# Attention and a routed MLP on one core: half-seen key tiles made in quarters of the array and packed into shared columns

## The chip, the cores and the metric

The kernel runs on one core of one Trainium2 chip. The metric is the device time of one execution in microseconds, the median of three runs. Engines are named as the profile names them: PE (TensorE, matmuls; its weight loads are PEld), DVE (VectorE), ACT (ScalarE), POOL (GpSimd) and SP (SyncE, which issues DMAs).

## What is computed

The first half is causal attention by blocks of 64: a query sees every key of its own block and of the blocks before it. There are 8 batches of 8 heads, 576 positions (9 blocks) and 64 dimensions.

```python
scores = scale * np.matmul(q, k.transpose(0, 1, 3, 2))
mask = block_i >= block_j
scores = np.where(mask, scores, -1000000000.0)
scores = scores - np.max(scores, axis=-1, keepdims=True)
attn = np.exp(scores)
attn = attn / (np.sum(attn, axis=-1, keepdims=True) + 1e-09)
return np.matmul(attn, v).astype(np.float32)
```

The second half takes the 4608 rows of 512 numbers that result. A gate chooses one of 8 experts for each row (a second, local gate can let a row keep the expert of the row before it), and the row goes through that expert's two matrices with a ReLU between, times the gate's share. The change touches the attention only.

## The kernel before

**Work items.** The attention walks over 32 pairs of heads (one batch, two heads). The two heads of a pair lie side by side: head 0's dimensions on partitions 0 to 63, head 1's on 64 to 127. So a matmul of queries and keys uses 64 rows of the array, and the two heads' matmuls run in its two row halves at the same time.

**Two sorts of scores.** For each pair the scores are made twice. First in bf16 with queries on partitions (`top`, three jobs: middle, high, low blocks), only for each query's maximum, which DVE takes from PSUM (L594, L597, L599). The maxima, negated, go on diagonals `diag` (L613, L620; one block of 64 columns for each block of queries). Then in f32 with keys on partitions: `products` (L650) makes scores transposed, and `less` (L659) subtracts each query's maximum by a matmul of `ones` with `diag`. `expo` (L666) takes the exponential on ACT into `prob`, and `av` (L684, L692) multiplies `prob` with V, two column halves of the array at a time, 65 columns each (64 of V, and a column of ones that gives the sum).

**Segments.** Keys come in five tiles of 128 (the last of 64). Key tile j needs only queries from 128 j on, so its columns number 576, 448, 320, 192 and 64: 1600 for each head. `SEGS` packs them into four segments, one PSUM tile of two banks each (one bank for each head). An entry is (key tile, first query, number, column): segment 0 holds tile 1 and tile 4, segment 1 the first 256 queries of tile 0 and tile 3, segment 2 tile 2, segment 3 the rest of tile 0. `place(j, q0)` finds a column in `prob` again.

**Half-seen tiles.** The first 64 queries of key tiles 0 to 3 belong to an even block, whose queries see only the first half of the tile's 128 keys. Before the change the whole tile is computed, and `corners` (L676) then sets the lower half of these 64 columns to zero, with four POOL memsets for a pair.

**Order of the work.** The order on every engine is written out by hand, in one loop over `it`. In one pass of it pair e = `it` gets its last two segments and V's products, pair c = e + 1 its middle and high maxima and its first two segments, pair a = e + 2 is transposed (`turns`, L987), and pair x = e - 1 has its result normalized (`norm`, L543, L544) and transposed (`halves_x`, L712). PE's order in one pass is: middle scores of c, segments 3 and 2 of e, turns of a, high scores of c, products of c's segments 0 and 1, transposes of x's result and of a's last block (L1044), low scores of a, subtractions for c (L659), V's products of e.

**PSUM tiles.** Three tiles of two banks serve all scores and segments; `seg_tile(place)` asks for one of three places. Places 1 and 2 change roles after every pass (`ring`). Place 0 holds c's middle scores and then c's segment 0, so these products wait until DVE has taken the middle maximum. Two single banks (`g_tile`) hold transposes and V's results; ACT copies the transposes out (L1053, L716, L720) before V's products take the bank again.

POOL holds, in its own order: exchanges of maxima (L607 to L609), low diagonals (L613), casts of queries into `qh` (L1028, L1069, L1072), the memsets, a cast of the result (L515) and the issues of the weights' DMAs (L63).

Of the kernel before, what the change touches and what calls it, by code (L numbers as in the profile page):

```python
# [16 lines left out]
def kernel(  # L17
# [11 lines left out]
    nc = tc.nc  # L29
# [16 lines left out]
    P = 128  # L46
# [352 lines left out]
    def slots(inv, tok_g, tok_s):  # L399
# [4 lines left out]
        if tok_s is not None:  # L404
# [13 lines left out]
    def place(j, q0):  # L418
        for s, parts in enumerate(SEGS):
# [18 lines left out]
    with tc.manual_schedule():  # L438
# [188 lines left out]
        def mid_maxima(i, where):  # L627
            top(i, 1, where)
            exchange(i, slice(5, 6), slice(6, 7), slice(12, 13))
            if i > 1:  # L630
                first_shift(i)

        def high_maxima(i, where):
# [6 lines left out]
            if i <= 1:  # L640
                first_shift(i)
# [20 lines left out]

        def expo(i, ps, s):
            p = prob[i % 2]
            w = sum(x[2] for x in SEGS[s])
            nc.scalar.activation(p[:, :, SEG0[s]:SEG0[s] + w], ps[:, :, 0:w],  # L666
                                 func=AF.Exp, scale=scale_attn)
            if s < 2:
                corners(i, s)

        def corners(i, s):
            p = prob[i % 2]
            for (j, a, n, c) in SEGS[s]:
                if j < 4 and a == 128 * j:
                    cc = SEG0[s] + c
                    nc.gpsimd.memset(p[64:128, :, cc:cc + 64], 0.0)  # L676

        def av(i, g, m):
# [9 lines left out]
            for h in range(2):  # L688
                for j in range(m + 1):
                    for e in range(2):  # L690
                        c = place(j, 128 * m + 64 * e)
                        nc.tensor.matmul(g[rows(e), o + 65 * h:o + 65 * h + 65],  # L692
                                         lhsT=p[:, h, c:c + 64], rhs=t[:, j, h, :],
# [279 lines left out]
        for it in range(-2, NPR):  # L973
# [24 lines left out]
            def segment(s, where):  # L998
                ps = seg_tile(where)
                products(e, ps, s, 0)  # L1000
                less(e, ps, s, 0)
                expo(e, ps, s)
# [27 lines left out]
            def tails():  # L1030

                tail = nat[:, 8].rearrange("p h d -> p (h d)") if on_a else None
                if on_x:
                    if it < NPR - 2:
                        g0, g1 = gx = g_tile(0), g_tile(1)
                    else:
                        ps = seg_tile(1 if on_c else 0)
# [45 lines left out]
            if it == -2:  # L1083
# [5 lines left out]
                top(0, 2, 1)  # L1089
                low_exchange(0)  # L1090
                weights(2)
                mid_maxima(0, 2)
# [3 lines left out]
                products(0, opened, 0, 1)  # L1096
                high_maxima(0, 1)
                continue

            if on_x:  # L1100
# [6 lines left out]
            if it == 0:  # L1107
                segment(3, 1)
                mid_maxima(c, 0)
                turns()  # L1110
                segment(2, 2)
            elif on_e:
                if on_c:
                    mid_maxima(c, 0)
                run(it, "mid")
                segment(3, 1)
                segment(2, 2)
# [18 lines left out]
            if on_e:  # L1136
                corners(e, 2)
            run(it, "begin")
            if on_c and not on_e:
                ps0, ps1 = opened, seg_tile(2)  # L1140
                for z in range(2):
                    products(c, ps1, 1, z)
                top(a, 2, 1)
# [262 lines left out]
```

## Time and profile before

| | us |
|---|---|
| runs: median of 3 (lowest, highest) | 452.41 (451.03, 453.89) |
| the profiled execution's own time | 456.63 |
| its span in the profile | 454.9 |
| start of the attention's last product with V (L692) | 304.6 |
| three ordinary pairs, 60.96 to 86.51 | 8.52, 8.52, 8.51 |

The granted clock was 0.996 of full speed over the span. In a timeline row the columns are start, duration of the merged group, engine, line, operation, tiles written and read, shapes, count, and in brackets the idle time of the engine before it with what ended it. A line of the profile that begins with a time range gives for each engine its busy time in that window and the number of its instructions, then the clock, the DMA share and GB/s. Matmuls of different parts of the array overlap, so their durations don't add; the distances between starts do.

### The profile page before, as it was taken

Reading aid. Unit: us, or ns where it says so; the run is one execution under the profiler, and the core shown is the slowest. Engines: PE = TensorE matmul, PEld = TensorE weight load, DVE = VectorE, ACT = ScalarE, POOL = GpSimd, SP = SyncE. Lnnn points to the kernel's source line nnn. Section 1 sums busy time; section 2 is a strip of 40 time slices with the busy share of each in tenths; the row PEclk is TensorE's granted clock in tenths of the full one; section 3 lists DMA queues with packets and bytes.
Section 4 is the critical chain, followed back from the end, with each engine's and each line's share of the span. In section 5 each row is a group of like instructions: output and inputs, shape, how many; then the busy total and the mean of one; then the engine's idle time right before and its main releaser. Section 6 shows DMA issues by size and latency. Waiting matters only on the chain. (4 is left out here: it accounts for less than half of the span.)

```text
span 454.9 us, 19769 instructions
## 1 busy us (share of the span) xinstructions
PE 429.3 (94%) x7780; PEld 338.4 (74%) x7802; DVE 316.4 (70%) x843; ACT 271.5 (60%) x573; POOL 295.5 (65%) x700
## 2 busy tenths in 40 slices
PE   7899899999999999899999999999999999999994
PEld 5688688878787877788778887786776676766772
DVE  4777667768778788887899998866865873333322
ACT  3856666766567757775777576454554553553552
POOL 4556466657556666887566788654877767667652
PEclk8999999999999999999999999999999999999999
DMA  7999799899999987999889998857545545555551
GB/s 153 187 164 173 138 177 184 157 186 171 184 171 171 170 167 149 194 157 180 172 167 178 163 192 145 143 107 161 139 131 154 143 124 155 146 123 156 138 122 66
DMA packets 169887, 71.18 MB, mean 156 GB/s; under 512 B 151424, under 2 KB 158080, under 8 KB 169792
## 3 DMA queue, kind: packets, MB, share of 16 engines
q1 hardware_dynamic: 154640, 38.05, 43.3%
q0 software_dynamic: 13952, 31.52, 34.4%
q8 instruction: 65, 1.06, 1.0%
q10 hardware_dynamic: 1200, 0.30, 0.3%
q14 instruction: 30, 0.25, 0.2%
HBM read 67.18 MB, written 14.97 MB: 181 GB/s over the span
## 5 line engine op out<-in xcount | busy, mean ns | idle before, releaser
L666 ACT ACTIVATE prob<-ps_s 128x640 f32<-128x640 f32 (+2 forms) x128 | 103.7, 839 | 44.1 <-PE ps_s L659 42.9
L594 DVE TENSOR_REDUCE mx<-ps_m 128x2 f32<-128x640 f32 (+2 forms) x96 | 100.3, 1044 | 17.5 <-PE ps_m L589 6.4
L650 PE MATMUL ps_s<-plb 64*128 64x320 f32 (+4 forms) x768 | 104.9, 394 | 1.2 <-DVE mx L597 0.9
L650 PEld LDWEIGHTS ps_s<-plb 64*128 64x128 f32 x768 | 69.2, 188 | 22.5 <-issue 11.1
L692 PE MATMUL g<-vt,prob 128*64 128x65 f32 x2560 | 81.1, 222 | 0.5 <-issue 0.4
L692 PEld LDWEIGHTS g<-vt,prob 128*64 128x64 f32 x2560 | 77.9, 138 | 1.0 <-issue 0.9
L827 ACT ACTIVATE hT<-ps_h 128x512 bf16<-128x512 f32 x76 | 43.9, 596 | 42.5 <-PE ps_h L823 28.4
L838 PE MATMUL ps_o<-w_bf,hT 128*128 x282 | 67.1, 379 | 1.4 <-issue 0.3
L838 PEld LDWEIGHTS <-hT 128*128 128x128 bf16 x304 | 28.0, 98 | 27.9 <-issue 0.3
L804 DVE COPY natb<-w_bf 128x4096 bf16 x20 | 24.7, 1236 | 30.9 <-PE ps_h L823 23.7
L841 ACT ACTIVATE o_sb<-ps_o,share 128x512 f32<-128x512 f32 x37 | 25.4, 687 | 29.5 <-PE ps_o L838 12.0
L804 DVE COPY plb<-w_bf 128x4096 bf16 x20 | 24.7, 1234 | 23.3 <-PE ps_h L823 13.7
L823 PEld LDWEIGHTS <-plb 128*128 128x128 bf16 x608 | 35.4, 98 | 7.0 <-issue 2.9
L823 PEld LDWEIGHTS <-natb 128*128 128x128 bf16 x608 | 35.4, 98 | 7.0 <-issue 2.3
L659 PE MATMUL ps_s<-diag,ones 64*128 64x448 bf16 (+1 forms) x372 | 36.7, 274 | 1.1 <-DVE diag L613 0.6
L63 POOL DMA_DIRECT2D w_bf<-in_moe_w_dram x56 | 34.1, 608 | 1.5 <-DMA x_rows<-xb 0.4
L1023 ACT COPY plb<-g 128x512 f32<-128x512 f32 x62 | 33.2, 593 | 1.2 <-PE g L987 1.2
L607 POOL COPY mx<-mx 64x2 f32<-64x2 f32 x64 | 11.7, 183 | 33.7 <-DVE mx L594 32.2
L676 POOL MEMSET prob<- 64x128 f32 x128 | 24.3, 205 | 13.1 <-ACT prob L666 7.6
L847 POOL DMA_INDIRECT out_dram<-o_sb,tok2s x17 | 19.0, 1117 | 20.0 <-ACT o_sb L841 10.9
L568 PE MATMUL ps_m<-kh,qh 64*128 64x320 bf16 (+2 forms) x192 | 25.7, 309 | 3.3 <-POOL qh L1028 1.2
L684 PEld LDWEIGHTS g<-vt,prob 128*64 128x64 f32 x640 | 21.4, 137 | 9.7 <-ACT xT L720 4.6
(291 smaller groups left out, 803.7 us busy)
## 6 DMA issues: line engine op xcount, KB each, us to landing
w_bf<-in_moe_w_dram POOLq DMA_DIRECT2D x48, 256.0 KB
vt<-in_v_dram SPq DMA_DIRECT2D x64, 128.0 KB
natb<-in_k_dram SPq DMA_DIRECT2D x63, 128.0 KB
natb<-in_q_dram SPq DMA_DIRECT2D x63, 128.0 KB
w_bf<-in_moe_w_dram POOLq DMA_DIRECT2D x8, 512.0 KB
x_rows<-w_bf SPq DMA_DIRECT2D x13, 256.0 KB
natb<-in_k_dram SPq DMA_DIRECT2D x32, 32.0 KB
vt<-in_v_dram SPq DMA_DIRECT2D x32, 32.0 KB
```

The costliest lines, as they stand in the source:

```text
L63: nc.gpsimd.dma_start(out=dst[:, e * WE:(e + 1) * WE].rearrange("p (k f) -> p k f", k=n)[:, r:r + m, :], in_=view[e][:, r:r + m, :])
L568: nc.tensor.matmul(ps[:, h, c:c + w], lhsT=qh[rows(h), 64 * b:64 * b + 128], rhs=kh[rows(h), 0:w], start=True, stop=m is None)
L594: nc.vector.reduce_max(mx[:, 7:12:4] if job == 0 else mx[:, b:b + 2], ps[:, :, 0:w], axis=AX)
L650: nc.tensor.matmul(ps[:, h, c:c + n], lhsT=pls[i][rows(h), S + 128 * j:S + 128 * j + 128], rhs=pls[i][rows(h), a:a + n], start=part == 0, ...
L659: nc.tensor.matmul(ps[:, h, c:c + n], lhsT=ones[rows(h), :], rhs=diag[rows(h), a // 64:(a + n) // 64, :], start=False, stop=part == len(SE ...
L666: nc.scalar.activation(p[:, :, SEG0[s]:SEG0[s] + w], ps[:, :, 0:w], func=AF.Exp, scale=scale_attn)
L692: nc.tensor.matmul(g[rows(e), o + 65 * h:o + 65 * h + 65], lhsT=p[:, h, c:c + 64], rhs=t[:, j, h, :], start=(j == 0), stop=(j == m))
L804: nc.vector.tensor_copy(w, w1_bf[:, bass.ds(off, WE)])
L823: nc.tensor.matmul(ps_h[:, f, :], lhsT=w[:, f0 + ko * F:f0 + ko * F + 2 * P - 1:2], rhs=xb[:, ko * P:(ko + 1) * P], start=(ko == 0), stop= ...
L827: nc.scalar.activation(hT[:, half * 4:half * 4 + 4, :], ps_h, func=AF.Relu)
L838: nc.tensor.matmul(ps_o, lhsT=hT[:, fo, :], rhs=w2_bf[:, bass.ds(woff + fo * Dm, Dm)], start=(fo == 0), stop=(fo == FO - 1))
L1023: nc.scalar.copy(pl[:, w * S:w * S + 512], pw[w])
```

## The change

`SEGS` has three segments instead of four, of 512, 512 and 448 columns for each head (1472 in all). The half-seen first 64 queries of key tiles 0 to 3 are no longer part of them. Blocks 0, 2, 4 and 6 are instead computed as 64 keys by 64 queries (`products_halves`, `less_halves`): blocks 0 and 2 write partitions 0 to 63, blocks 4 and 6 partitions 64 to 127, so that 0 and 4 share 64 columns and 2 and 6 the next 64 (`HALVES` lists block, half and column). With two heads in two row halves that is four quarters of the array.

V's products must then take from such a column only the half that belongs to their block. They use `vh`, a copy of V whose other half is zero: `halves_v` fills it for each pair with two POOL copies, at the start of the pass; there is one `vh` for all pairs. The memsets of `corners` are gone.

The halves are computed at the start of a pass, behind the V products of the pair before and ahead of the middle scores of c; the rest of segment 2 follows after these, in the same PSUM tile. `first_shift`, which makes the diagonal of block 0, moves for every pair to the end of `high_maxima`. The places of the three PSUM tiles change so that they need no exchange after every pass.

```diff
-    SEGS = [[(1, 128, 448, 0), (4, 512, 64, 448)],
-            [(0, 0, 256, 0), (3, 384, 192, 256)],
-            [(2, 256, 320, 0)],
-            [(0, 256, 320, 0)]]
-    SEG0 = [448, 0, 960, 1280]
-    WP = 1600
+    SEGS = [[(0, 64, 512, 0)],
+            [(1, 192, 384, 0), (3, 448, 128, 384)],
+            [(2, 320, 256, 0), (4, 512, 64, 384)]]
+    HALVES = [(0, 0, 256), (4, 1, 256), (2, 0, 320), (6, 1, 320)]
+    SEG0 = [0, 512, 1024]
+    WP = 1472
...
+        vh = const([P, 4, 2, D + 1], F32, "vh")
+        nc.gpsimd.memset(vh, 0.0)
+        for z in range(2):
+            nc.gpsimd.memset(vh[64 * z:64 * z + 64, 2 * z:2 * z + 2, :, D:D + 1], 1.0)
...
         def mid_maxima(i, where):
             top(i, 1, where)
             exchange(i, slice(5, 6), slice(6, 7), slice(12, 13))
-            if i > 1:
-                first_shift(i)
...
             shift(i, 7, 2, nc.vector)
-            if i <= 1:
-                first_shift(i)
+            first_shift(i)
...
+        def products_halves(i, ps):
+            for b, z, c in HALVES:
+                for h in range(2):
+                    nc.tensor.matmul(ps[rows(z), h, c:c + 64],
+                                     lhsT=pls[i][rows(h), S + 64 * b:S + 64 * b + 64],
+                                     rhs=pls[i][rows(h), 64 * b:64 * b + 64],
+                                     start=c == 256, stop=False)
+
+        def less_halves(i, ps):
+            diag = diag1 if i else diag0
+            for b, z, c in HALVES:
+                for h in range(2):
+                    nc.tensor.matmul(ps[rows(z), h, c:c + 64], lhsT=ones[rows(h), 0:64],
+                                     rhs=diag[rows(h), b, :], start=False, stop=c > 256)
...
-        def corners(i, s):
-            p = prob[i % 2]
-            for (j, a, n, c) in SEGS[s]:
-                if j < 4 and a == 128 * j:
-                    cc = SEG0[s] + c
-                    nc.gpsimd.memset(p[64:128, :, cc:cc + 64], 0.0)
+        def halves_v(i):
+            for z in range(2):
+                nc.gpsimd.tensor_copy(vh[rows(z), 2 * z:2 * z + 2, :, 0:D],
+                                      vt[i % 2][rows(0), 2 * z:2 * z + 2, :, 0:D])
...
-                                         lhsT=p[:, h, c:c + 64], rhs=t[:, j, h, :],
+                                         lhsT=p[:, h, c:c + 64],
+                                         rhs=(t if e or j < m else vh)[:, j, h, :],
...
+            if on_e:
+                halves_v(e)
...
             elif on_e:
+                ps = halves(1)
                 if on_c:
                     mid_maxima(c, 0)
                 run(it, "mid")
-                segment(3, 1)
-                segment(2, 2)
+                segment(ps)
...
-                    high_maxima(c, 1)
+                    high_maxima(c, 2)
...
-            if on_e:
-                corners(e, 2)
...
             if on_c and on_e:
-                ps0, ps1 = seg_tile(0), seg_tile(2)
+                ps0, ps1 = seg_tile(0), seg_tile(1)
                 products(c, ps0, 0, 0)
                 for z in range(2):
                     products(c, ps1, 1, z)
-                products(c, ps0, 0, 1)
```

PE's order in an ordinary pass, from the end of V's products to the next pair's products. `g` is a bank of V's results or transposes, `ps_m` scores for maxima, `ps_s` a segment. Of rows that come once for each head one is shown. Before:

```order
L692 MATMUL g_891<-vt_149,prob_147 64x65 x24
L583 MATMUL ps_m<-kh,qh 128x64
L589 MATMUL ps_m<-kh,qh 128x384
L650 MATMUL ps_s<-plb 128x320 x2
L659 MATMUL ps_s<-diag,ones 128x320
L987 MATMUL g_953<-id_f,natb 128x64
L568 MATMUL ps_m<-kh,qh 128x512
L650 MATMUL ps_s<-plb 128x448 x2
L650 MATMUL ps_s<-plb 128x256 x2
L650 MATMUL ps_s<-plb 128x192 x2
L650 MATMUL ps_s<-plb 128x64 x2
```

The rows of L650 and L659 with 320 columns come twice there, once for segment 3 and once for segment 2. After:

```order
L670 MATMUL ps_s<-plb 64x64 x8
L679 MATMUL ps_s<-diag,ones 64x64
L590 MATMUL ps_m<-kh,qh 128x64
L596 MATMUL ps_m<-kh,qh 128x384
L654 MATMUL ps_s<-plb 128x256 x2
L654 MATMUL ps_s<-plb 128x64 x2
L663 MATMUL ps_s<-diag,ones 128x256
L1003 MATMUL g_988<-id_f,natb 128x64
L575 MATMUL ps_m<-kh,qh 128x512
L654 MATMUL ps_s<-plb 128x512 x2
L654 MATMUL ps_s<-plb 128x384 x2
L654 MATMUL ps_s<-plb 128x128 x2
```

The halves (eight products, eight subtractions of L679) now stand between V's products and the middle scores; one segment of 320 columns is gone, and the next pair's products have three parts and 1024 columns instead of four parts and 960.

DVE's order in the same stretch, from the normalization of the result (`x<-g`) to the low maxima. Before:

```order
L543 RECIPROCAL rs<-g_1280 128x6
L544 TENSOR_TENSOR x<-g_1280,rs 128x384
L594 TENSOR_REDUCE mx<-ps_m 128x2
L599 TENSOR_REDUCE mx<-ps_m 128x2
L620 TENSOR_TENSOR diag<-negi,mx 64x64 x2
L594 TENSOR_REDUCE mx<-ps_m 128x2
L636 TENSOR_REDUCE mx<-mx 64x1
L637 COPY mx<-mx 64x1
L638 TENSOR_REDUCE mx<-mx 64x1
L613 TENSOR_TENSOR diag<-negi,mx 128x128
L594 TENSOR_REDUCE mx<-ps_m 128x2
```

After:

```order
L550 RECIPROCAL rs<-g_1317 128x6
L551 TENSOR_TENSOR x<-g_1317,rs 128x384
L601 TENSOR_REDUCE mx<-ps_m 128x2
L606 TENSOR_REDUCE mx<-ps_m 128x2
L601 TENSOR_REDUCE mx<-ps_m 128x2
L641 TENSOR_REDUCE mx<-mx 64x1
L642 COPY mx<-mx 64x1
L643 TENSOR_REDUCE mx<-mx 64x1
L620 TENSOR_TENSOR diag<-negi,mx 128x128
L627 TENSOR_TENSOR diag<-negi,mx 64x64 x2
L601 TENSOR_REDUCE mx<-ps_m 128x2
```

The two instructions for block 0's diagonal moved from between the middle and the high maximum to behind the high blocks' diagonal.

More of the change, by code (lines that the diff above doesn't have):

```diff
@@ L996, in weights, with halves, segment @@
                     n -= m
-            def segment(s, where):
+            def halves(where):
                 ps = seg_tile(where)
-                products(e, ps, s, 0)
-                less(e, ps, s, 0)
-                expo(e, ps, s)
+                products_halves(e, ps)
+                less_halves(e, ps)
+                return ps
+            def segment(ps):
+                for z in range(2):
+                    products(e, ps, 2, z)
+                for z in range(2):
+                    less(e, ps, 2, z)
+                expo(e, ps, 2)
             def turns():
@@ L1221 @@
                 keep_sums(x, ge)
-            if on_e:
-                ring[1:] = ring[:0:-1]
         att.close()
```

30 lines of the change are left out of this document (15 added, 15 removed).

## The prediction

> **What bounds the kernel now.** I read the engines' shares first, then the busy time of one ordinary pair of heads by windows, then the timeline of that pair for each engine. The page's first row:
>
> ```profile
> PE 429.3 (94%) x7780; PEld 338.4 (74%) x7802; DVE 316.4 (70%) x843; ACT 271.5 (60%) x573; POOL 295.5 (65%) x700
> ```
>
> TensorE (PE) looks full, but matmuls overlap and their ends are modelled, so the share alone proves little. The window of one ordinary pair of the attention, and PE's timeline in it:
>
> ```profile
> 69.48:78.00 8.52, 8.41 (x192) 7.04 (x186) 6.31 (x16) 5.94 (x13) 5.73 (x19) 1.00 1.08 187
> ```
>
> ```profile
> 68.80 0.87 PE L692 MATMUL g<-vt,prob 128*64 128x65 f32 x24
> 69.60 0.23 PE L583 MATMUL ps_m<-kh,qh 64*128 64x64 bf16 x4
> 69.67 0.19 PE L589 MATMUL ps_m<-kh,qh 64*128 64x64 bf16 x2
> 69.70 0.19 PE L563 MATMUL ps_m<-ones,unseen 64*128 64x64 bf16 x2
> 69.73 0.33 PE L589 MATMUL ps_m<-kh,qh 64*128 64x384 bf16 x2
> 69.89 0.70 PE L650 MATMUL ps_s<-plb 64*128 64x320 f32 x4
> 70.43 0.30 PE L659 MATMUL ps_s<-diag,ones 64*128 64x320 bf16 x2
> 70.57 0.70 PE L650 MATMUL ps_s<-plb 64*128 64x320 f32 x4
> ...
> 71.24 0.66 PE L987 MATMUL g<-id_f,natb 64*128 64x64 f32 x16
> 71.73 0.38 PE L568 MATMUL ps_m<-kh,qh 64*128 64x512 bf16 x2
> 71.95 1.84 PE L650 MATMUL ps_s<-plb 64*128 64x448 f32 x16
> 73.63 0.48 PE L712 MATMUL g<-id_f,x 64*128 64x64 f32 x10
> 73.94 0.23 PE L1044 MATMUL g<-id_f,natb 64*128 64x64 f32 x2
> ...
> 75.05 0.80 PE L684 MATMUL g<-vt,prob 128*64 128x65 f32 x20
> 75.69 2.50 PE L692 MATMUL g<-vt,prob 128*64 128x65 f32 x80
> 78.12 0.23 PE L583 MATMUL ps_m<-kh,qh 64*128 64x64 bf16 x4
> ```
>
> Starts are what counts here. From start to start: middle scores 0.29 us (69.60 to 69.89), segment 3 0.68, segment 2 0.67, turns 0.49, high scores 0.22, the next pair's products 1.68, turned results 0.31, then 1.11 to V's products, which take 3.07 until the next pair. I call 69.60 time 0 of the pair: products start at 2.35, L712 at 4.03, V's products at 5.45, the next pair at 8.52. PE is the bound nearly everywhere, with one wait inside that PE's speed can't shorten:
>
> ```profile
> 75.05 0.66 PEld L684 LDWEIGHTS g<-vt,prob 128*64 128x64 f32 x20 [0.37 <-ACT xT L720]
> ```
>
> ```profile
> 74.24 0.27 ACT L1053 COPY plb<-g 128x128 f32<-128x128 f32 x1 [0.55 <-PE g L1044]
> ...
> 74.79 0.21 ACT L720 COPY xT<-g 64x64 f32<-64x64 f32 x1
> ```
>
> V's products wait for a chain of ACT copies that starts only when L1044 is done. So the 1.11 us after L1044 are fixed, and the top scores and the subtractions in it (L659 of the next pair's segments) have 0.37 us to spare: 64 columns more there, about 0.03 us, cost nothing.
>
> The second thing to see is how close VectorE (DVE) stands behind PE:
>
> ```profile
> 69.72 0.20 DVE L543 RECIPROCAL rs<-g 128x6 f32<-128x6 f32 x1 [0.56 <-PE g L692]
> ...
> 70.42 1.08 DVE L594 TENSOR_REDUCE mx<-ps_m 128x2 f32<-128x896 f32 x1
> 71.42 0.28 DVE L599 TENSOR_REDUCE mx<-ps_m 128x2 f32<-128x128 f32 x1
> ```
>
> The next pair's products at 71.95 go into the PSUM tile (place 0) that these two maxima read, and L599 ends at 71.70: slack of a quarter of a microsecond. In a pair where the maxima came later, PE did wait:
>
> ```profile
> 233.81 1.08 DVE L594 TENSOR_REDUCE mx<-ps_m 128x2 f32<-128x896 f32 x1
> 234.81 0.28 DVE L599 TENSOR_REDUCE mx<-ps_m 128x2 f32<-128x128 f32 x1
> ```
>
> ```profile
> 235.15 0.30 PEld L650 LDWEIGHTS ps_s<-plb 64*128 64x128 f32 x4 [0.27 <-DVE mx L599]
> 235.63 0.19 PEld L650 LDWEIGHTS ps_s<-plb 64*128 64x128 f32 x2 [0.18 <-issue]
> ```
>
> From the start of L594 to the first product are 235.15 - 233.81 = 1.34 us, and the first pass then takes 0.48 instead of 448 x 0.84 ns = 0.38, since its weights were not loaded ahead: 0.10 on top. The view of the products' tile counts four such waits before the change:
>
> ```profile
>   DVE mx L599: 1.5, 4
> ```
>
> **The change, part by part.** Prices first. A pass of 320 f32 columns by both heads at once is half of 70.43 - 69.89 = 0.54, or 0.84 ns a column; bf16 takes 70.57 - 70.43 = 0.14 for 320, or 0.43 ns.
>
> *Removed:* segment 3 (0.68), and of segment 2's 0.67 what shrinks: now 256 + 64 columns, twice 320 x 0.84 = 0.54, and 0.14 to subtract. To that 0.07 for the narrow part: the 960 columns at 71.95 should take 1.61 and take 1.68, and I put the rest down to the 64-column part, whose weights are as wide as any (an estimate). That part moves to segment 2. Segment 2 then costs 0.75.
>
> *Added:* the halves, 8 f32 matmuls (16 passes) and 8 bf16 of 64 columns, in quarters of the array. No row shows a 64x64 quarter. The two-at-a-time step is known: V's products, 65 columns, take 0.058 each two ((0.87 - 0.22) / 11 from the first row), and 64 bf16 columns 0.03. One at a time would be 16 x 0.058 + 8 x 0.03 = 1.17 us, two at a time 0.58, four at a time 4 x 0.058 + 2 x 0.03 = 0.29. The nearest row is the gate's sums, which put four column groups into the array:
>
> ```profile
> 95.22 0.63 PE L757 MATMUL g<-xT,wgl 128*32 128x128 f32 x14
> ...
> 95.98 0.53 PE L757 MATMUL g<-scr,wgl 128*32 128x128 f32 x6
> 96.44 0.23 PE L583 MATMUL ps_m<-kh,qh 64*128 64x64 bf16 x4
> ```
>
> Between the first and the last row shown stand 32 passes, 16 of 160 and 16 of 128 columns. Two at a time they would need 1.94 us (288 x 16 x 0.84 / 2); they took 1.22. So four do run together, and the two heads' row groups do as well: I take 0.29 and keep 0.58 for the range.
>
> *Changes of the array's shape.* V's last 24 passes at 68.80 need 12 x 0.059 = 0.71 and the next start is 69.60: 0.10 lost when the shape goes from 128x64 to 64x128. The halves put a third shape between, so this is paid twice: 0.10 more (bounds 0 and 0.10). [...] The first f32 step after a change also costs 0.05 (20 passes at 75.05 take 0.64, ten steps of 0.059 are 0.59).
>
> *What that makes of a pair.* Halves from 0 to 0.05 + 0.29 = 0.34; change, so middle scores at 0.44. How soon can DVE take their maximum? At 70.42 it was DVE that was late, with its normalization. Where DVE was free:
>
> ```profile
> 96.94 1.09 DVE L594 TENSOR_REDUCE mx<-ps_m 128x2 f32<-128x896 f32 x1 [0.89 <-PE ps_m L589]
> ```
>
> That is 0.50 after the scores' start at 96.44. So the maximum starts at the later of 0.82 (DVE free, 70.42) and 0.44 + 0.50 = 0.94: PE now is late by 0.12. Products at 0.94 + 1.34 = 2.28, plus 0.10 for weights not ahead, in effect 2.38 against 2.35. PE itself would have been ready at 0.44 + 0.29 + 0.75 + 0.49 + 0.22 = 2.19, so the columns that were saved turn into a wait of 0.09 and the 0.10 behind it. The products are now 512 + 384 + 128 = 1024 columns, 2 x 1024 x 0.84 = 1.72, without the 0.07. L712 starts at 4.10 against 4.03: a pair takes 0.07 us longer. Bounds: with maxima at 0.82 (shape changes free) products at 2.26, a pair 0.05 shorter; with halves at 0.58, 0.36 longer.
>
> *Hidden or small.* The exponentials fall from 3200 to 2944 columns and from four to three instructions a pair; ACT waits for PE there and gives nothing back:
>
> ```profile
> 70.77 1.44 ACT L666 ACTIVATE prob<-ps_s 128x640 f32<-128x640 f32 x2 [1.96 <-PE ps_s L659]
> ```
>
> POOL loses four memsets (three take 0.66) and gains two copies of 64x256, bounded by its rows of 128 and 640 columns:
>
> ```profile
> 71.64 0.18 POOL L607 COPY mx<-mx 64x1 f32<-64x1 f32 x1 [1.20 <-DVE mx L594]
> ...
> 73.24 0.61 POOL L1028 CAST qh<-plb 128x512 bf16<-128x512 f32 x1
> ...
> 75.47 0.30 POOL L1072 CAST qh<-plb 128x128 bf16<-128x128 f32 x1
> ...
> 76.29 0.73 POOL L515 CAST w_bf<-x 128x640 bf16<-128x640 f32 x1
> 77.08 0.66 POOL L676 MEMSET prob<- 64x128 f32 x3
> ```
>
> 0.30 to 0.73 each, 0.4 by size. They wait for V's last product of the pair before, since they overwrite `vh`, and block POOL's queue so long: behind them stands L607, which waits for DVE until 71.64 anyway (1.20 idle), so 0.8 us is covered. Where POOL makes one-hot rows in that gap (two pairs) I count 0.2 each. Block 0's diagonal (two DVE instructions) leaves the path from middle to high maximum, which helps only where PE waited for the diagonal, as here:
>
> ```profile
> 183.53 0.59 PE L659 MATMUL ps_s<-diag,ones 64*128 64x448 bf16 x8 [0.30 <-DVE diag L613]
> ```
>
> I allow 0.2 each for two such pairs, beyond what the fixed ACT chain would hold PE for anyway (an estimate); it cancels POOL's 0.4. No DMA is added; only weights' issues on POOL come earlier by the memsets. First and last pairs cancel within 0.3.
>
> **Sum.** 29 pairs x 0.07 = +2.0 us on a profiled span of 454.9 (the run itself took 456.6). That is +0.4%; carried to the median of the runs, 452.4 + 2.0 = 454.4.
>
> **The rivals.** *B, slower: quarters go two at a time.* Then halves take 0.58, scores start at 0.73, the maximum at 1.23, and a pair grows by 0.36: 29 x 0.36 = 10.4, 462.8 us. It decides once the halves take over 0.38 us (0.16 a pair, 29 of which make 4.6). For it: no row mixes row and column groups. Against it: L757. [...]
>
> *C, the saving arrives.* If products need not wait for the maximum, they start at 2.19 and a pair loses 2.35 + 1.68 - 2.19 - 1.72 = 0.12: 29 x 0.12 = 3.5, 448.9 us. Against it stands the wait at 235.15, on this very tile.
>
> *D, POOL takes over.* L1028 ends at 73.85 and top scores start at 74.00; with maxima 0.12 later it ends at 73.97 and PE wants it at 74.07. Another 0.2 us on POOL would show fully: 0.17 a pair, 29 x 0.17 = 4.9, 457.3 us.
>
> **How the numbers follow.** My forecast 0.58, B 0.19, C 0.10, D 0.13. The forecast's own range runs from -0.05 to +0.16 a pair, 450.9 to 457.0. Eight in ten over all: 449.0 to 462.5. A measurement of this kernel can tell about 1% from no change. Faster by over 1% (below 447.9) needs more than C gives: 0.07. Slower by over 1% (above 456.9): B, over half of D and the edge of the forecast, 0.30. Within 1%: 0.63.
>
> **What would show it.** Right: a row of PEld at the next pair's products that waits for the DVE maximum in nearly every pair (instead of four); middle maxima waiting for PE; halves that span about 0.3 us of starts; 0.1 us between shapes; an ordinary pair of 8.55 to 8.6 us. Wrong: a pair under 8.45, or no wait at the products; halves over 0.38 us; top scores that wait for POOL's `qh` in every pair.

## The result, and the profile after

| | before | after |
|---|---|---|
| runs, us: median (lowest to highest) | 452.32 (451.03 to 453.89), 4 | 464.77 (463.72 to 466.45), 4 |
| ratio, 95% interval | | 1.0293 (1.0253 to 1.0333) |
| profiled execution, its span | 456.63, 454.9 | 466.45, 464.7 |
| three ordinary pairs | 8.52, 8.52, 8.51 | 8.67, 8.67, 8.67 |

The change makes the kernel 2.9% slower, 12.4 us; the forecast was 454.4, and 462.5 the end of its range. From the page after, the engines' shares and three of the DMA queues (packets, MB, share of 16 engines):

```profile
PE 434.3 (93%) x8356; PEld 343.4 (74%) x8378; DVE 318.2 (68%) x843; ACT 261.1 (56%) x541; POOL 300.8 (65%) x639
...
q1 hardware_dynamic: 154640, 38.05, 43.2%
q0 software_dynamic: 13952, 31.52, 34.1%
q8 instruction: 69, 1.13, 1.1%
```

ACT has become 10 us less busy and PE is busy 5 us longer, with 576 matmuls and 576 weight loads more. An ordinary pair, PE in the timeline (from the halves on; rows of single matmuls left out):

```profile
83.24 0.46 PE L670 MATMUL ps_s<-plb 64*64 64x64 f32 x16
83.52 0.24 PE L679 MATMUL ps_s<-diag,ones 64*64 64x64 bf16 x8
83.70 0.23 PE L590 MATMUL ps_m<-kh,qh 64*128 64x64 bf16 x4
...
83.99 0.76 PE L654 MATMUL ps_s<-plb 64*128 64x256 f32 x8
84.58 0.30 PE L663 MATMUL ps_s<-diag,ones 64*128 64x256 bf16 x4
84.72 0.69 PE L1003 MATMUL g<-id_f,natb 64*128 64x64 f32 x16
85.25 0.38 PE L575 MATMUL ps_m<-kh,qh 64*128 64x512 bf16 x2
85.63 2.00 PE L654 MATMUL ps_s<-plb 64*128 64x512 f32 x12
87.43 0.50 PE L728 MATMUL g<-id_f,x 64*128 64x64 f32 x10
87.73 0.26 PE L1067 MATMUL g<-id_f,natb 64*128 64x64 f32 x2
...
88.84 0.80 PE L699 MATMUL g<-vt,prob 128*64 128x65 f32 x20
```

The same pair on DVE, and PE's weight loads at the next products:

```profile
84.19 1.09 DVE L601 TENSOR_REDUCE mx<-ps_m 128x2 f32<-128x896 f32 x1
85.20 0.28 DVE L606 TENSOR_REDUCE mx<-ps_m 128x2 f32<-128x128 f32 x1
```

```profile
85.60 0.33 PEld L654 LDWEIGHTS ps_s<-plb 64*128 64x128 f32 x4 [0.30 <-PE g L1003]
86.13 0.22 PEld L654 LDWEIGHTS ps_s<-plb 64*128 64x128 f32 x2 [0.21 <-ACT prob L685]
```

With 83.24 as time 0, the middle scores start at 0.46, the maximum at 0.95, the products at 2.39 and L728 at 4.19; from L1067 to V's products are 1.11 us as before. The weight load at 85.60 stands behind DVE's L606, which ends at 85.48: the trace names another releaser, and the time tells the right one. All of that is the forecast's picture, 0.09 us too late at its end (L728 at 4.19, forecast 4.10). But 29 pairs of +0.155 are 4.5 us, and the kernel lost 12.4. The rest is in single passes. The view of the waits (who waits for whom: us in all, times, longest) shows what before had only in small (there the cast of `qh`, L1028, made PE's weight loads wait 3.1 us in five waits, the longest 1.2):

```profile
POOL vh L690 <- DMA vt<-in_v_dram: 11.1, 3, 5.5
PEld L575 <- POOL qh L1051: 10.5, 5, 4.7
PE ps_m L575 <- POOL qh L1051: 8.6, 3, 4.6
```

And one such place in the timeline, POOL first, then PE:

```profile
38.96 0.82 POOL L690 COPY vh<-vt 64x256 f32<-64x256 f32 x2 [5.52 <-DMA vt<-in_v_dram]
...
41.27 0.60 POOL L1051 CAST qh<-plb 128x512 bf16<-128x512 f32 x1
```

```profile
38.38 0.26 PE L1067 MATMUL g<-id_f,natb 64*128 64x64 f32 x2
41.93 0.31 PE L575 MATMUL ps_m<-kh,qh 64*128 64x320 bf16 x2 [3.28 <-POOL qh L1051]
...
42.90 1.35 PE L699 MATMUL g<-vt,prob 128*64 128x65 f32 x20
```

V's copies stand at the head of POOL's queue for the pass and wait 5.52 us for V to land. Behind them stand the exchange of maxima and the cast of `qh` (L1051), and PE's low scores (L575) wait for that cast for 3.28 us; at 285.27 the same costs 4.56 us. V was late from its start, too. SyncE had issued the last part of V's transfer only at 33.75, when POOL was ready for it at 33.44:

```profile
33.14 0.61 SPq L517 DMA_DIRECT2D vt<-in_v_dram  x1
```

In the pass of the wait at 285.27 the issue ended 1.6 us before POOL was ready. The product with V that follows the first of the two waits takes 1.35 us for the 20 matmuls that take 0.80 at 88.84, and the window there says why (its last three figures are the clock, the DMA share and GB/s):

```profile
42.50:45.90 3.40, 3.40 (x62) 0.50 0.82 143
```

The granted clock was 0.50 for 3.41 us after each of the two long idles (3.28 and 4.56 us), by an estimate from that rate and length 1.7 us more each. In the first experiment below the clock fell to 0.50 behind a wait of only 1.42 us.

In all tables below, the stretch is the time from the start of the first pair's products with V (L699; L684 in before) to the start of the 29th pair's, read in one profiled execution: 255.0 us in before, 265.2 after. It leaves out what comes behind the 29th start.

### The profile page after: what moved, and what is told of

Read it like the earlier page. It is cut to its first block, busy times and chain, and to the rows that moved or that the text cites. A ratio compares the mean times of both kernels' runs of the same rounds, so it can differ in the third digit from the quotient of the medians.

```text
span 464.7 us, 20760 instructions
## 1 busy us (share of the span) xinstructions
PE 434.3 (93%) x8356; PEld 343.4 (74%) x8378; DVE 318.2 (68%) x843; ACT 261.1 (56%) x541; POOL 300.8 (65%) x639
## 3 DMA queue, kind: packets, MB, share of 16 engines
q8 instruction: 69, 1.13, 1.1%
## 4 chain that ended last, share of the span: by engine, by line
PE 56%; DMA 11%; POOL 11%; issue 9%; DVE 5%; ACT 5%; SPq 1%; POOLq 1%; DVEq 0%; ACTq 0%
PE ps_s L654 14%; PE g L707 14%; POOL out_dram L863 6%; DMA vt<-in_v_dram 5%; PE g L699 5%; PE ps_h L839 4%; DMA out_dram<-o_sb,tok2s 3%; PE ps_o L854 3%; PE g L1003 3%; PE ps_s L670 2%; PE g L773 2%; DMA scr<-scr 2%; PE ps_m L575 2%; PE g L728 2%; PE ps_s L663 1%
## 5 line engine op out<-in xcount | busy, mean ns | idle before, releaser
L685 ACT ACTIVATE prob<-ps_s 128x1024 f32<-128x1024 f32 (+1 forms) x96 | 91.4, 990 | 67.8 <-PE ps_s L663 67.8
L654 PE MATMUL ps_s<-plb 64*128 64x64 f32 (+4 forms) x640 | 90.4, 405 | 1.9 <-DVE mx L606 0.8
L654 PEld LDWEIGHTS ps_s<-plb 64*128 64x128 f32 x640 | 63.6, 188 | 31.8 <-issue 8.1
L707 PEld LDWEIGHTS g<-vt,prob 128*64 128x64 f32 x2048 | 79.0, 140 | 0.7 <-issue 0.7
L843 ACT ACTIVATE hT<-ps_h 128x512 bf16<-128x512 f32 x76 | 45.2, 597 | 25.8 <-PE ps_h L839 25.5
L707 PE MATMUL g<-vh,prob 128*64 128x65 f32 x512 | 58.7, 222 | 0.3 <-ACT prob L685 0.3
L707 PEld LDWEIGHTS g<-vh,prob 128*64 128x64 f32 x512 | 45.4, 139 | 0.4 <-issue 0.4
L690 POOL COPY vh<-vt 64x256 f32<-64x256 f32 x64 | 25.2, 394 | 21.5 <-DMA vt<-in_v_dram 11.1
L575 PE MATMUL ps_m<-kh,qh 64*128 64x320 bf16 (+2 forms) x192 | 26.8, 311 | 10.1 <-POOL qh L1051 8.6
L863 POOL DMA_INDIRECT out_dram<-o_sb,tok2s x17 | 28.3, 1665 | 12.1 <-ACT o_sb L857 7.2
```

What stands on the lines that cost most here:

```text
L575: nc.tensor.matmul(ps[:, h, c:c + w], lhsT=qh[rows(h), 64 * b:64 * b + 128], rhs=kh[rows(h), 0:w], start=True, stop=m is None)
L654: nc.tensor.matmul(ps[:, h, c:c + n], lhsT=pls[i][rows(h), S + 128 * j:S + 128 * j + 128], rhs=pls[i][rows(h), a:a + n], start=part == 0, ...
L707: nc.tensor.matmul(g[rows(e), o + 65 * h:o + 65 * h + 65], lhsT=p[:, h, c:c + 64], rhs=(t if e or j < m else vh)[:, j, h, :], start=(j == ...
L843: nc.scalar.activation(hT[:, half * 4:half * 4 + 4, :], ps_h, func=AF.Relu)
L863: wr = nc.gpsimd.indirect_dma_start(out=out_flat, out_offset=bass.IndirectOffsetOnAxis(ap=g[1][:, g[3]:g[3] + 1], axis=0), in_=o_sb, in_of ...
```

## The experiments

Theory V says that the excess comes from V's copies, which need V's transfer earlier in the pass than the products do. Theories M and P are about the ordinary pair: the wait for the middle maximum, against what the changes of shape cost. Theory O is that the added instructions cost time whatever else happens. Theory I came later: PE's own instructions arrive late.

**The copies moved behind the turned queries and keys.**

```diff
-            if on_e:
-                halves_v(e)
...
             if on_a:
                 halves_in()
+            if on_e:
+                halves_v(e)
```

> The two copies of V's halves stand behind the cast of the queries on POOL instead of at the start of the pass. Theory V (the copies wait for V's DMA at the head of POOL's queue, and everything behind them, the queries' cast above all, comes late): the waits of the low scores for the cast of 3.5 and 4.7 us go, ordinary pairs stay at 8.67 us, and the time falls by 7 to 10 us to about 455 to 458. Rival D (the DMA itself is late for all, so that the wait only moves): V's products or the low scores wait instead, by the same 3 to 5 us in the same two passes, and the time stays above 462.

465.48 us (462.41 to 467.81), ratio 1.0267 (1.0200 to 1.0334). POOL no longer waits for V between 20 and 300 us, the long waits for `qh` are gone (0.6 us at most), and yet the median did not fall. So V's copies alone don't explain the excess. They are not cleared by it either: the stretch fell to 257.5, and the passes that were long were others. The longest stands right behind the stretch: 13.73 us from the 29th start to the 30th, where the changed kernel without loads (below) takes 10.05. It holds a wait of PE that the profile does not explain, and the half clock behind it:

```profile
286.03 0.20 PE L663 MATMUL ps_s<-diag,ones 64*128 64x64 bf16 x2 [1.42 <-issue]
```

```profile
287.14:290.55 3.41, 3.41 (x16) 1.95 (x14) 2.52 (x7) 1.65 (x4) 1.48 (x3) 0.50 0.45 95
```

**The middle scores ahead of the halves.**

```diff
-                ps = halves(1)
                 if on_c:
                     mid_maxima(c, 0)
+                ps = halves(1)
```

> The middle scores stand ahead of the halves again; one more change of the array's shape in each pass (about 0.10 us). Theory M (an ordinary pair is longer because the middle maximum starts 0.12 us late and the next pair's products wait for it): the middle maximum starts 0.82 us after V's products again, no wait before the next products, an ordinary pair falls from 8.67 to about 8.50 us, 29 pairs give 5 us, about 460. Rival P (a pair is longer because PE has more to do in it): a pair grows by the change of shape to about 8.77, about 468.

465.31 us (462.05 to 469.66), ratio 1.0298 (1.0234 to 1.0362). One pair of its timeline:

```profile
62.08 0.23 PE L590 MATMUL ps_m<-kh,qh 64*128 64x64 bf16 x4
...
62.46 0.46 PE L670 MATMUL ps_s<-plb 64*64 64x64 f32 x16
62.74 0.24 PE L679 MATMUL ps_s<-diag,ones 64*64 64x64 bf16 x8
62.91 0.87 PE L654 MATMUL ps_s<-plb 64*128 64x256 f32 x8
...
64.28 0.38 PE L575 MATMUL ps_m<-kh,qh 64*128 64x512 bf16 x2
64.50 1.89 PE L654 MATMUL ps_s<-plb 64*128 64x512 f32 x12
```

The products follow the high scores after 0.22 us, as in before: the wait for the maximum is gone. An ordinary pair takes 8.63 us, not 8.50. The halves now stand between two jobs of the other shape, and both changes are paid, the second with a weight load that was not ahead (L654 takes 0.87 where it took 0.76). So the saved columns are spent on changes of shape instead of on a wait: both theories hold half, and neither order brings the pair under 8.51.

**Both edits together.**

> Both moves together. If theories V and M both hold, their gains add: 465 less 8 to 10 less 5, about 450 to 453, equal to the kernel before within 1%. If either rival holds, 458 or more.

461.76 us (460.02 to 466.15), ratio 1.0220 (1.0148 to 1.0292). A pair takes 8.63; POOL waits for V 0.4 us in all. The ordinary pairs now explain 29 x 0.12 = 3.5 us, and the waits of theory V are gone, but 5 to 6.5 us are left (8.4 us over its companion by the medians, 10 by the ratio). The two gains do not add up to the kernel before.

**The halves' order in the text.**

```diff
-    HALVES = [(0, 0, 256), (4, 1, 256), (2, 0, 320), (6, 1, 320)]
+    HALVES = [(0, 0, 256), (2, 0, 320), (4, 1, 256), (6, 1, 320)]
```

> The changed kernel with the order of the four halves altered, so that two blocks that use the same quarters follow each other (0, 2, then 4, 6). If PE starts matmuls in program order and a quarter takes one at a time, only two run together: the halves' starts span about 0.55 to 0.6 us instead of 0.33, and since the middle scores come behind them an ordinary pair grows by about 0.25 us, 7 us in all, about 472. If PE picks what a free quarter can take, nothing changes: 465.

466.17 us (464.77 to 469.71), ratio 1.0309 (1.0246 to 1.0373). An ordinary pair takes 8.69, 0.02 more, and the four quarters still start together, 7 to 20 ns apart. So this run didn't bring quarters one after the other, and says nothing on what that would cost; what kept them together, the order in the stream or the hardware, stays open.

**No copies at all**, the half-seen columns' share left out of the sum. The edit drops the call of `halves_v`.

> The changed kernel without the two POOL copies of a pass: the copy of V's halves stays zero, so the half-seen columns add nothing to the result. Theory V (beyond 0.155 us in each ordinary pair, the time goes where POOL's copies wait for V's DMA): these waits and their followers are gone, ordinary pairs stay at 8.67 us, and the time is that of the kernel before plus 29 x 0.155 = 4.5 us, 457 to 459. Theory O (the copies are not it; the loads or the end of the attention are late for another reason): 462 or more.

460.76 us (455.77 to 461.11), ratio 1.0211 (1.0140 to 1.0283): by the ratios the copies cost 0.8%, some 3.7 us, by the medians 1.9 us (10.5 over its companion, against 12.4), and the interval meets that of the change. So most of the excess is left without them, and the time lies between what theories V and O expected. Long waits stand in the middle of runs of PE's instructions, put down to "issue", which is time for which the profile shows no reason.

**No copies, and the middle scores first.**

> The middle scores ahead of the halves and no copies, so that the half-seen columns add nothing. What is left of the change is then PE's own work and its changes of shape: ordinary pairs of 8.63 us, 29 x 0.12 = 3.4 us over the kernel before, 456 to 458 by theory V; 460 or more by theory O.

459.24 us (457.55 to 463.17), ratio 1.0242 (1.0176 to 1.0309), again between the two theories. Again pairs of 8.63, and again waits that nothing explains:

```profile
32.73 0.28 PE L707 MATMUL g<-vt,prob 128*64 128x65 f32 x3 [0.64 <-issue]
...
39.94 0.21 PE L663 MATMUL ps_s<-diag,ones 64*128 64x128 bf16 x1 [0.96 <-issue]
...
258.30 0.34 PE L1003 MATMUL g<-id_f,natb 64*128 64x64 f32 x3 [0.62 <-issue]
```

**Before and after once more**, unchanged.

> The kernel before once more, to see how much of a profile's time is its own: ordinary pairs of 8.51 us again in any case. If the stalls of the first profile (1.35 us for the queries' load, 0.4 to 1.2 us for the queries' cast in five pairs) belong to the kernel they come in the same pairs; if they are chance of the DMA they move.

> The changed kernel once more: ordinary pairs of 8.67 us again. Theory V: POOL's copies wait for V's DMA again, 6 to 11 us in all over the run, in other passes than before.

450.56 and 462.3 us. Before's few stalls stand mostly in the same passes as in its first profile (stretch 254.3 against 255.0), so most are its own. The changed kernel's move: stretch 261.3, POOL waits for V eight times, 2.9 us at most, in other passes than before, and one of the unexplained waits is 1.63 us long, between two products with V that wait for nobody:

```profile
172.40 0.28 PE L707 MATMUL g<-vt,prob 128*64 128x65 f32 x3 [1.63 <-issue]
```

*What these waits have in common.* I numbered PE's recorded instructions (weight loads, matmuls, waits, register operations) in order of time. In ten profiles of kernels with the loads in place, two of before and eight of changed ones, the attention has 28 waits over 0.2 us at a number that is 193 to 197 modulo 256. That is five places in 256, yet all the waits shown above as "issue" stand there (numbers 961, 1217, 11458, 7361, and 12738 in the first experiment). The two profiles of before have none. Packets of the instruction queue q8 carry 16 KB each, 65 packets for before's 16176 recorded instructions, 69 for the changed kernel's 17359, which is 249 and 252 instructions to a packet. If the instructions from one number that is 193 modulo 256 to the next are called a block, exactly one packet starts in each of the attention's blocks, 49 in the first profile of before and 51 in the first of the changed kernel. And each such wait ends 1.3 to 1.7 us after a packet has landed. So I read q8 as PE's program, a packet for each block of 256. The wait shown in the first experiment is met at the same place of the stream in seven of the eight profiles of changed kernels, 0.5 to 1.7 us long, in the pass behind the stretch.

So a block's packet can be read from the trace like any transfer. With the loads in place a packet starts 1.4 to 1.8 us (medians of the profiles; at most 5.6) after PE has entered the block ahead of it, takes about 1.1 (0.9 to 2.1), and 1.3 us or more go by until PE enters the next block: about 4.2 us in all, an estimate from these three. By theory I PE stands still where a block lasts less than that, and what delays the packets is the other transfers. The next runs take a large part of these away, the loads of the experts' weights (48 of 256 KB and 8 of 512, 16.8 MB; the 31.5 MB of the next expectation are all that their queue moves).

**The weights loaded at the end of pass 30**, in before, in the changed kernel, and in the variant without copies.

```diff
-                weights(2)
...
-            if on_e:
-                weights({0: 0, 28: 2, 29: 2}.get(it, it < 28 and it not in none))
...
-            weights({-1: 2, 0: 2, 28: 2, 29: 2}.get(it, it < 28 and it not in none))
+            if it == 30:
+                weights(len(quarters) - 2)
```

> The kernel before, with the experts' weights loaded in one go at the end of pass 30 and no longer a little in every pass (the first experts' pairs wait for them, so the whole becomes longer, by something like the 31.5 MB at the 170 to 190 GB/s that the profile of before moves: 100 to 180 us; only differences between this run and its two companions count). What the three are for: in the profiles of the changed kernels the waits of TensorE for nothing that the profile shows fall, all of them over 0.25 us but those on a named semaphore, on instructions whose number is 193 to 197 modulo 256, and the queue of instruction packets brings TensorE's program in packets of 16 KB, one for 256 instructions; each such wait ends 1.3 to 1.6 us after a packet has landed. Theory I (instruction packets come late): a packet is asked for when a block of 256 is begun, waits 1 to 6 us behind the weights' and rows' packets and lands too late when the block is short in time; the changed kernel has 36 more instructions in each pass, 48 of them in a third of a microsecond, so it is met far more often. It expects here: no such wait (as in before, where none is over 0.25 us), packets that start sooner, and the attention from the first to the twenty-ninth product with V at 253 to 255 us as before (254.3 and 255.0), or up to 2 us less. Rival O (the added instructions cost time in places of their own, whatever the transfers do) expects the same of this kernel.

> The changed kernel with the weights loaded at the end of pass 30. Its attention from the first to the twenty-ninth product with V took 265.2 and 261.3 us, against 255.0 and 254.3 of before. Theory I, with theory V (POOL's copies wait for V's transfer), both of which hang on the same crowded transfer engines: the waits at instruction 193 modulo 256 go, V lands sooner, and what is left are the ordinary pairs, 28 x 0.155 = 4.3 us: 3.5 to 5.5 us over the companion of before on this stretch, and 3.5 to 6 us in the time of the whole. Rival O: 7 to 10 us on the stretch as with the loads, and 9 to 13 us in the whole.

> The changed kernel with the middle maximum's columns ahead of the halves and without V's copies (what the half-seen columns add is left out of the sum), and with the weights loaded at the end of pass 30. With the loads in every pass its stretch took 258.6 us, 4.0 over before, and 8 to 9 us more in the whole, of which its ordinary pairs explain 28 x 0.12 = 3.4. Theory I: no wait at instruction 193 modulo 256 any more, 3 to 4.5 us over the companion on the stretch and 3 to 5 us in the whole. Rival O: 5 us or more on the stretch with waits that are put down to nothing still in the middle of the products with V, and 7 to 9 us in the whole.

| stretch, us | loads in every pass | loads at the end |
|---|---|---|
| before | 255.0, 254.3 | 249.5 |
| changed | 265.2, 261.3 | 252.4 |
| middle first, no copies | 258.6 | 251.1 |

Until the loads begin no wait is left at 193 modulo 256, none of POOL for V, and the packets start after 0.5 to 0.7 us (medians). The difference on the stretch falls to 2.9 us and 1.6, each under what theory I expected (3.5 and 3 at least) and far under theory O (7 and 5). Before gains as well, 5 us: the crowding was there, and the change about doubled its price. The whole times (529.64, 537.84 and 540.34) missed what was expected, since the time in which PE stands still for the loads behind pass 30, 77 to 86 us, differs from kernel to kernel: they can't be compared. One of the four executions of the changed kernel took 911.04 us (the median holds it); there is no profile of it, and the cause stays open.

**Before with 36 more PE instructions a pass.**

```diff
+                for n in range(18):
+                    w, c = n % 2, n // 2 % 2
+                    nc.tensor.matmul(pw[w][64 * c:64 * c + 64, 0:1],
+                                     lhsT=ones[rows(w), 0:64], rhs=ones[rows(w), 0:1],
+                                     start=True, stop=True)
                 for b in range(8):
                     turn_pair(b)
```

> The kernel before, loads as they were, with 18 more products of one column in every pass ahead of the turns (ones by ones, into a quarter of the array in turn, written over by the turns), so 36 more TensorE instructions a pass, the number that the change adds. Their own time is visible in the ordinary pair (0.15 to 0.5 us by the 7 to 25 ns that small products took apart in the traces, and up to 0.2 for two changes of shape), so 4 to 15 us over 29 pairs. Theory I: beside it the kernel before now shows waits of 0.3 us and more at instructions of one number modulo 256 (where its own profiles show none), four or more of them, 2 to 5 us together. Rival O: the pairs are longer, and no such waits appear.

465.92 us (463.26 to 468.37), ratio 1.0203 (1.0136 to 1.0270). The pair grew by 0.40, which is 11.6 us for 29 and more than all of the loss, and only one wait stands at 193 modulo 256 (0.48 us). Theory I's numbers failed here, and the run came out nearer to theory O: it isn't the count of instructions. The 18 products took a quarter of a microsecond and two changes of shape, so the blocks did not get shorter in time. The shortest lasted 4.33 us; of before's 49, two were under 4.2, of after's some 50, ten.

**No loads at all**, so that whole times compare: zeros in the weights' tiles, and so in the experts' result.

```diff
+    nc.vector.memset(w1_bf, 0.0)
+    nc.gpsimd.memset(w2_bf, 0.0)
...
-        at(31, "end", lambda ps: weights(2))
+        at(31, "end", lambda ps: nc.gpsimd.memset(w2_bf[:, E * WE - WE // 2:], 0.0))
```

The other calls of `weights` are dropped too.

> The kernel before without any load of the experts' weights (zeros are written into their tiles at the start, by VectorE and GpSimd, and the experts' result is zero), so that its whole time can be compared with its companion's, which the loads at the end of pass 30 did not allow. Its own time: 20 to 40 us more at the start, the attention's stretch from the first to the twenty-ninth product with V at 249 to 250 us (249.5 with the loads late).

> The changed kernel without any load of the weights, zeros in their place. If the excess of the change over its ordinary pairs is made by the crowded transfer engines (V landing late for POOL's copies, instruction packets late), the stretch is 2.5 to 4.5 us over the companion, as with the loads late (252.4 against 249.5), and the whole time 2 to 5 us over it, against 12.4 with the loads. If the added instructions and copies cost time whatever the transfers do, the whole time is 8 us or more over the companion's.

473.04 us (472.63 to 473.51) and 476.57 us (476.35 to 477.56), six executions each, none of which overlap: 3.5 us. That is the change's own price, and theory O falls: 12.4 - 3.5 = 8.9 us (8 to 12 by the interval of the ratio) come only with the loads. Four windows of 50 us (busy time by engine, clock, DMA share, GB/s): before, before without loads, after, after without loads.

```profile
150.00:200.00 50.00, 48.07 (x1032) 39.17 (x1028) 41.89 (x116) 33.07 (x74) 35.95 (x113) 1.00 0.92 171
```

```profile
150.00:200.00 50.00, 49.27 (x1113) 40.84 (x1110) 40.42 (x116) 33.84 (x80) 27.09 (x98) 1.00 0.51 118
```

```profile
150.00:200.00 50.00, 48.22 (x1102) 38.94 (x1100) 41.59 (x117) 32.85 (x76) 35.36 (x100) 1.00 0.89 162
```

```profile
150.00:200.00 50.00, 49.09 (x1153) 40.35 (x1151) 40.73 (x114) 32.12 (x77) 26.71 (x81) 1.00 0.51 118
```

The transfer engines go from 0.9 busy to 0.51. The difference of the two kernels by pass is now bare: +0.15 or +0.16 in most, -0.05 to -0.09 in three, -0.27 to -0.55 in three; 2.8 us by the attention's last products. Blocks of 256 instructions under 4.2 us number 2 of 46 in before and 13 of 50 after. The 34 us in which POOL issued the loads are gone as well, so for V's copies its own relief can't be told from that of the transfers. PE's packets have a queue of their own (q8, in after 69 packets, all of 16 KB), and every DMA that the trace shows POOL issuing moves a tensor of the kernel. V is also issued earlier without the loads: SyncE is done with it 2.3 to 8 us before POOL is ready, with them as late as 0.3 us after.

**The same program, 96 instructions further on.** The variant without copies, with 48 products of one column put once ahead of the first pair's turns.

```diff
                 if a == 0:
+                    for n in range(48):
+                        w, c = n % 2, n // 2 % 2
+                        nc.tensor.matmul(pw[w][64 * c:64 * c + 64, 0:1],
+                                         lhsT=ones[rows(w), 0:64], rhs=ones[rows(w), 0:1],
+                                         start=True, stop=True)
```

> The changed kernel with the middle maximum's columns ahead of the halves and without V's copies (what the half-seen columns add is left out of the sum), as in an earlier run, with 48 products of one column (96 TensorE instructions) put once ahead of the first pair's turns, so that every later instruction stands 96 places further in TensorE's stream. If the waits in the middle of runs of products are waits for the next packet of 256 instructions, they fall on other lines than before but again on numbers 193 to 197 modulo 256, in the count from the start; the time differs from the earlier run's ratio of 1.0242 by no more than its interval. If they belong to the lines, they fall on the same lines and passes as before, on numbers 33 to 37 modulo 256.

457.34 us (453.00 to 463.37), ratio 1.0155 (1.0082 to 1.0228). Two waits over 0.2 us are left of that kind, on numbers 1474 and 5313, 194 and 193 modulo 256 in the new count, where the earlier run had waits at 961, 1217, 1475 and so on of the old one:

```profile
41.52 0.22 PE L707 MATMUL g<-vt,prob 128*64 128x65 f32 x1 [0.52 <-issue]
...
123.03 0.28 PE L707 MATMUL g<-vt,prob 128*64 128x65 f32 x3 [0.36 <-issue]
```

The waits belong to the place in the stream and not to the lines. The ratio lies just under the earlier interval, so that part of the expectation was missed, and the profile has 0.9 us of such waits instead of 5.0; that where the boundaries fall matters this much is suggested by one profile each, not shown.

## Why the prediction was wrong, point by point

- **PE, DVE and the fixed ACT chain: right.** PE waits for the middle maximum in ordinary pairs, the chain behind L1067 still takes 1.11 us, the exponentials that were saved give nothing back, and the columns saved ahead of the products turn into a wait.
- **The quarters: right.** All four run together: the 16 passes span 0.28 us of starts up to L679, and with the 8 small ones and the change of shape it is 0.46 up to the middle scores (0.44 forecast). Rival B falls. A change of shape cost about 0.10, as read (the last L679 starts at 83.57, the first L590 at 83.70, and 64 bf16 columns are 0.03 of that).
- **The size of a pair: missed.** It grew by 0.155, not 0.07, the upper edge of the forecast's own range. The term is the way from the maximum to the first product. The maximum started at 0.95 (0.94 forecast), the first product 1.44 later; the forecast had 1.34 from the row at 235.15, where the load came 0.06 us after L599's end and not 0.12 (85.48 to 85.60). What makes that difference stays open. The second load cost 0.08, where 0.10 was paid for it. 29 x 0.155 would be 4.5; since six passes got shorter the attention differs by 2.8 us in the kernels without loads, and with 0.7 outside of it that is their 3.5. Forecast: 2.0.
- **"Hidden or small": the step that failed.** The sum holds the ordinary pair alone and puts nothing for waits on transfers; 8.9 of the 12.4 us came only with the loads. I wrote that the copies wait "for V's last product of the pair before", that they block POOL's queue "so long" and "0.8 us is covered". The wait that the traces show is another: V's own transfer. Before, V was needed by the products 5.45 us into the pass; the copies need it at the start. With transfer engines 0.9 busy, it had not landed in three passes of one profile and in eight of another (11 us of POOL's time in each). Rival D named the place (POOL late with the queries' cast), but priced it as 0.2 us in every pair. It came as 1 to 5 us in a few.
- **"No DMA is added": true and beside the point.** By the packets of q8 (1.13 MB after) PE's program is itself a transfer. The change makes its 256-instruction blocks shorter in time (48 instructions in the halves' third of a microsecond; ten blocks under 4.2 us, where before has two). The profiles of before have no wait over 0.2 us at their borders; in those of the changed kernel such waits make 1.3 and 3.7 us.
- **The frame of the sum.** "29 pairs x 0.07" takes every pass for an ordinary one. The price fell on the passes in which something was late already. By the profiles, V's copies and PE's packets share the 8.9 us in portions that change from one execution to the next: PE waited for the cast behind the copies 8.6 us in one profile and 4.4 in the other, for its packets 1.3 and 3.7. How they divide in the median stays open. That the run with the copies moved (the first) was no faster, and the one without copies was by 1.9 to 3.7 us, fits this, and does not prove a split.

## What to carry to other kernels

An operation that moves a need for a transfer to an earlier place in a queue has to be priced against the landing of that transfer, with all that stands behind it, even if no transfer is added (here POOL waited 11 us for V in each of two profiles, and PE behind it up to 4.56 us at once). Where transfer engines are as busy as here, 0.9, look for the stalls of single passes and not only at the ordinary one, and take the crowding away once (loads late or left out) to see a change's own price. Many small instructions in a short time can have a price beside their own duration: here waits of 0.2 to 1.7 us where a block of 256 begins.

## What the runs showed of the hardware

- Queue q8 carried 65 packets of 16 KB in before and 69 after, one in each block of 256 of PE's recorded instructions (49 of 49 and 51 of 51 in the attention). The way of a packet, from PE's entry into a block to the earliest entry into the next, was about 4.2 us with transfer engines 0.9 busy (1.8 + 1.1 + 1.3), and about 3.1 with 0.5 (0.7 + 1.1 + 1.3): estimates from the figures above. PE stood still for 0.2 to 1.7 us at 28 block borders in ten profiles, until 1.3 to 1.7 us after a packet had landed.
- 64x64 quarters, two row halves by two column halves, started 7 ns apart and stepped together at 58 ns for 64 f32 columns, after a first step of 0.11 us (after, from 83.24: 16 passes in 0.28 us).
- The granted clock fell to 0.50 for 3.41 us behind waits of 3.28 and 4.56 us, and in another profile behind one of 1.42 us.
- 18 products of one column with as many weight loads, in four quarters, took about 0.25 us (109.49 to 109.74 in the run with 36 more instructions a pass); with the two changes of shape around them a pair became 0.40 us longer.
